# The last three rows of W_down, loaded by GpSimd in nine unequal transfers

## The chip, the cores and the metric

The kernel runs on one core of one Trainium2 chip. The metric is the device time of one execution in microseconds (us). The kernel before takes 383.76 us, the median of three runs (383.7 to 384.0).

## The reference, cut to what matters

One decode step of a transformer layer for 4 sequences, with model width 576: a layer norm, attention of 32 query heads on 16 cached key/value heads over a window of 4096 positions, a residual, a second layer norm, and a gated feed-forward layer of width 4608. What the change touches is the last matrix product of the feed-forward layer:

```python
gate = jnp.einsum("bsd,df->bsf", x, W_gate)
up = jnp.einsum("bsd,df->bsf", x, W_up)
gate = gate * (gate > 0)
h = gate * up
return jnp.einsum("bsf,fd->bsd", h, W_down)   # W_down: 4608 x 576, bf16
```

All arrays are bf16. Keys, values and weights together are 159.6 MB, and each byte is read once.

## The kernel before, in words

The kernel is written engine by engine. A small scheduler (`Sched`, L50 to L100) turns names into semaphore counts: `op` and `dma` wait for the names in `deps` and announce their own. Each engine's program runs in the order in which it is written: `prog_sync` (L267), `prog_pool` (L275), `prog_act` (L299), `prog_dve` (L366) and `prog_pe` (L516). TensorE (PE) records all matmuls under L520, since a helper `mm` issues them.

**Loads.** All large loads stand in one list, `transfers`, and SyncE (SP) issues them in that order on one queue (L268). The order is wq, then 32 pairs of K and V tiles of 2 MB each, then wo, W_gate and W_up, and last W_down. A transfer waits only for the consumers of the part of the SBUF tile `pool` that it overwrites. Each covers all 128 partitions.

**W_down.** Partition p holds 36 rows of W_down, numbered f = 0 to 35, of 576 elements (1152 bytes) each: four groups of nine (`NG` = 4, `JJ` = 9). The list `WD` (L251) cuts the 36 rows into nine transfers, `("wd", 0)` to `("wd", 8)`: two of 9 rows, five of 3 rows, one of 2 rows and one of 1 row. A row over all partitions is 144 KB. They are issued at L256, and their only condition is `"ATTN"`, the last matmul of the output projection, because W_down takes the place of wo in `pool`.

**After the loads.** PE computes gate and up from W_gate and W_up as they land. ScalarE (ACT) applies the relu (L361), VectorE (DVE) multiplies and transposes the product into `hhT` (L507 and L510, names `("HHT", g)` for group g). Then PE takes the W_down transfers in the order of `WD` (L660): for each row f two matmuls of 288 columns, one for each half of the 576 outputs, all into one accumulator bank. The very last one, `"DOWN1"`, releases two copies, one on ACT (L363) and one on DVE (L513), and SP stores the result (L270).

**GpSimd (POOL).** It sets constants at the start and does one maximum over all partitions for each of eight batches of the attention (L295). Behind the eighth its program is empty, and it issues no transfer. ACT issues one small transfer, that of x, at L301.

Of the kernel before, what the change touches and what calls it, by code (L numbers as in the profile page):

```python
# [13 lines left out]
D = 576  # L14
# [7 lines left out]
FC = F // 128  # L22
# [17 lines left out]
JJ = 9  # L40
BIG = 1.5e38
NG = FC // JJ
# [60 lines left out]
def bass_sequential_preLN__sliding_block_cached__glu_gated_reglu__decode_kernel(  # L103
# [12 lines left out]
    with ExitStack() as es:  # L116
        cnt = [0]

        def sb(name, shape, dt):
            return es.enter_context(nc.sbuf_tensor(name, shape, dt))  # L120

        pool = sb("pool", [128, (NKS + NVS) * DUO], BF16)
# [69 lines left out]
        S = Sched()  # L192
# [45 lines left out]
        for g in range(NWO):  # L238
            add(("wo", g), f"wo{g}", g * ROW, ROW, "ATTN",
                lambda e, o, g=g: e.dma_start(out=o,  # L240
                                              in_=A_wo[g * 1024:(g + 1) * 1024, :].rearrange("(p e) n -> p (e n)", e=8)))
# [6 lines left out]
                lambda e, o, W=W: e.dma_start(out=o, in_=W[512:576, :].rearrange("r (u n) -> (r u) n", u=2)))  # L248

        wd_sb = pool[:, 0:FC * D].rearrange("p (g x) -> p g x", g=NG)  # L250
        WD = [(0, 9), (9, 18), (18, 21), (21, 24), (24, 27), (27, 30), (30, 33), (33, 35), (35, 36)]  # L251
        for k, (f0, f1) in enumerate(WD):
            g0, j0 = divmod(f0, JJ)
            g1, nj = (f1 // JJ, JJ) if f1 - f0 >= JJ else (g0 + 1, f1 - f0)
# [2 lines left out]
                                  out=wd_sb[:, g0:g1, j0 * D:(j0 + nj) * D],  # L257
                                  in_=B_W_down[g0 * 128 * JJ:g1 * 128 * JJ, :].rearrange("(g p j) n -> p g (j n)", p=128, j=JJ)[:, :, j0 * D:(j0 + nj) * D])))

        def feat(c):  # L260
            return slice(c // 2 * 256 + c % 2, c // 2 * 256 + c % 2 + 255, 2) if c < 4 else slice(512, D)

        def land(name):
            return ("L",) + (name if isinstance(name, tuple) else (name,))
# [9 lines left out]

        def prog_pool(S):  # L275
            g = "gpsimd"
            S.op(g, lambda e: e.memset(eps_c[:, :], EPS), name="EPS")
            S.op(g, lambda e: e.memset(ident_b[:, :], 0.0), name="P0")
            S.op(g, lambda e: e.memset(qz[:, :, :, :, :].rearrange("p a r c m -> p (a r c m)"), 0.0), name="QZ0")
            S.op(g, lambda e: e.affine_select(out=ident_b[:, :], in_=ident_b[:, :], pattern=[[-1, 128]],  # L280
                                              compare_op=ALU.not_equal, fill=1.0, base=0, channel_multiplier=1),
                 deps=["P0"], name="IDB")
            S.op(g, lambda e: e.memset(ones_f[:, :], 1.0), name="ONES")
            S.op(g, lambda e: e.memset(R_sb[:, :, :, :], 0.0), name="R0")
            S.op(g, lambda e: e.memset(hnT[:, :, :], 0.0), name="HNZ")
            S.op(g, lambda e: e.memset(hn4[:, :, :], 0.0), name="HN4Z")
            S.op(g, lambda e: e.memset(ident_f[:, :], 0.0), name="P1")
            S.op(g, lambda e: e.affine_select(out=ident_f[:, :], in_=ident_f[:, :], pattern=[[-1, 128]],
                                              compare_op=ALU.not_equal, fill=1.0, base=0, channel_multiplier=1),
                 deps=["P1"], name="IDF")  # L290
            for n in range(NBATCH):
                deps = [("EMAX", n)]
                if n >= 2:
                    deps.append(("BIAS", n - 2))
                S.op(g, lambda e, n=n: e.partition_all_reduce(bcm[:, n % 2, :], pmax[:, n % 2, :], 128, bass_isa.ReduceOp.max),  # L295
                     deps=deps, name=("PAR", n))


        def prog_act(S):  # L299
# [216 lines left out]
        def prog_pe(S):  # L516
            t = "tensor"

            def mm(o, l, r, start, stop, deps=(), name=None, skip=False):
                S.op(t, lambda e: e.matmul(o, lhsT=l, rhs=r, start=start, stop=stop, skip_group_check=skip),  # L520
                     deps=deps, name=name, signal=name is not None)

            for k, (src, base) in enumerate(((xn_bf, 0), (x_bf, 32))):
                for c in range(DC):
                    w = 128 if c < 4 else 64
                    last = k == 1 and c == DC - 1
                    S.op(t, lambda e, c=c, w=w, src=src, base=base: e.transpose(  # L527
                        out=tpv[0:w, base + c * 4:base + (c + 1) * 4], in_=src[0:B, feat(c)], identity=ident_b[0:B, 0:B]),
                        deps=["A_XN", "IDB", land("x")] if k == 0 and c == 0 else [], name="TP1" if last else None, signal=last)
            mm(pb[STB][:, 0:B], dup[:, :], x4[:, :], True, True, deps=["D_XNT", "DUP"], name="XDUP")  # L530
            first = True
            for c in range(4):
                s = at[("wq", c // 2)] + (c % 2) * HQ
                for h in range(H):
                    mm(pb[QB][:, h * B:(h + 1) * B], pool[:, s + h * DH:s + (h + 1) * DH], xnT[:, c, :], first, False,
                       deps=[land(("wq", c // 2))] + (["D_XNT"] if first else []) if h == 0 else [], skip=True)
                    first = False
            s = at[("wq", 4)]
            for h in range(H // 2):
                o = pb[QB][:, 0:H * B].rearrange("p (u x) -> p u x", u=2)[:, :, h * B:(h + 1) * B]  # L540
                mm(o, pool[:, s + h * DH:s + (h + 1) * DH], xn4[:, :, :], False, h == H // 2 - 1,
                   deps=[land(("wq", 4)), "XN41"] if h == 0 else [],
                   name="QMM" if h == H // 2 - 1 else None, skip=True)
            for ce in range(4):
                mm(pb[QR][:, ce * 128:(ce + 1) * 128], sel[:, ce, :, :].rearrange("p g k -> p (g k)"), qT_sb[:, :], True, True,
                   deps=["D_QT", "SEL3"] if ce == 0 else [], name="QREP" if ce == 3 else None)
# [55 lines left out]
            for e_ in range(8):  # L602
                mm(sc[:, e_ * 128:(e_ + 1) * 128], S8[:, e_ * 128:(e_ + 1) * 128], oT_all[:, :, :].rearrange("p h b -> p (h b)"), True, True,
                   deps=[("NORM", b) for b in range(B)] + ["S8"] if e_ == 0 else [], name="OSEL" if e_ == 7 else None)
            for g in range(NWO):
                wv = pool[:, at[("wo", g)]:at[("wo", g)] + ROW].rearrange("p (e n) -> p e n", e=8)
                deps = [land(("wo", g))] + (["D_OX"] if g == 0 else [])
                for n in range(DC):
                    w = 128 if n < 4 else 64
                    for e_ in range(8):  # L610
                        last = g == NWO - 1 and n == DC - 1 and e_ == 7
                        mm(pb[WOB][0:w, n * B:(n + 1) * B], wv[:, e_, feat(n)], oX[:, e_, g, :],
                           g == 0 and n == 0 and e_ == 0, last, deps=deps, name="ATTN" if last else None, skip=True)
                        deps = []
# [19 lines left out]
            for c in range(4):  # L634
                if c == 2:
                    residual()
                for u, kind in ((0, "wg"), (1, "wu")):
                    s = at[(kind, c // 2)] + (c % 2) * F
                    deps = [land((kind, c // 2))] + (["N2"] if c == 0 and u == 0 else [])
                    begun = set()  # L640
                    for g, f0, f1, bank, c0 in PARTS:
                        for q in range(4):
# [3 lines left out]
                            deps = []  # L646
                        begun.add(bank)

            for u, kind in ((0, "wg"), (1, "wu")):
                s = at[(kind, 4)]  # L650
                deps = [land((kind, 4)), "HN41"]
                for k, (g, f0, f1, bank, c0) in enumerate(PARTS):
                    for q in range(4):
                        x0 = s + (g % 2) * 4 * JW + q * JW
                        last = k >= 2
                        mm(pb[GUB[u][bank]][32 * q:32 * q + 32, c0:c0 + (f1 - f0) * JJ], hn4[:, g // 2, :], pool[:, x0 + f0 * JJ:x0 + f1 * JJ],
                           False, last, deps=deps, name=(("GATE", "GU")[u], bank) if last and q == 3 else None, skip=True)
                        deps = []

            for k, (f0, f1) in enumerate(WD):  # L660
                deps = [land(("wd", k))]
                for f in range(f0, f1):
                    g, j = divmod(f, JJ)
                    if f % JJ == 0:
                        deps = deps + [("HHT", f // JJ)]
                    for u in range(2):
                        last = f == FC - 1
                        mm(pb[DNB][32 * u:32 * u + B, 0:HD], hhT[:, f, 0:B], wd_sb[:, g, j * D + u * HD:j * D + (u + 1) * HD], False, last,
                           deps=deps, name="DOWN1" if last and u == 1 else None, skip=True)
                        deps = []  # L670

        progs = [("gpsimd", prog_pool), ("sync", prog_sync), ("scalar", prog_act), ("vector", prog_dve), ("tensor", prog_pe)]
        S.begin(False)
        for _, p in progs:
# [33 lines left out]
```

## Time and profile before

| what | value |
|---|---|
| median of three runs | 383.76 us |
| the profiled execution | 383.99 us |
| its span, first to last instruction | 382.2 us |
| read from HBM | 159.58 MB, 418 GB/s over the span |
| PE busy | 287.7 us (75%) |
| DVE busy | 206.5 us (54%) |
| ACT busy | 53.5 us (14%) |
| POOL busy | 8.2 us (2%) |
| the eight maxima on POOL, the last at | 310.38 us |
| "ATTN" releases the W_down transfers at | 347.2 us |

Times within the profile are microseconds from the start of the span. The profiled execution is 0.23 us longer than the median of the runs, and 1.8 us of it lie outside the span. The page shows the core's 16 DMA engines together, as the mean share of time in which they were busy; the trace holds one record for each packet that a DMA engine moved (one partition's piece of a transfer is a packet here), and one for each increment of a transfer's semaphore. A transfer on 128 partitions increments its semaphore 16 times, once for each DMA engine that has moved its part, and the consumer waits for all 16. The records name the queue of a packet but not the number of the DMA engine.

### The profile page before, as it was taken

Reading aid. Unit: us, or ns where it says so; the run is one execution under the profiler, and the core shown is the slowest. Engines: PE = TensorE matmul, PEld = TensorE weight load, DVE = VectorE, ACT = ScalarE, POOL = GpSimd, SP = SyncE. Lnnn points to the kernel's source line nnn. Section 1 sums busy time; section 2 is a strip of 40 time slices with the busy share of each in tenths; the row PEclk is TensorE's granted clock in tenths of the full one; section 3 lists DMA queues with packets and bytes.
Section 4 is the critical chain, followed back from the end, with each engine's and each line's share of the span. In section 5 each row is a group of like instructions: output and inputs, shape, how many; then the busy total and the mean of one; then the engine's idle time right before and its main releaser. Section 6 shows DMA issues by size and latency. Waiting matters only on the chain.

```text
span 382.2 us, 3916 instructions
## 1 busy us (share of the span) xinstructions
PE 287.7 (75%) x1697; PEld 124.5 (33%) x1712; DVE 206.5 (54%) x193; ACT 53.5 (14%) x129; POOL 8.2 (2%) x22
## 2 busy tenths in 40 slices
PE   0069749977997799669967996799589796956565
PEld 0053213322432243224322432243224233344331
DVE  0369789369437854774477548744865442042030
ACT  4021050021102110211021103010300021010020
POOL 4100000000000000000000000000000000000000
PEclk9999988997998799989998999899989996965677
DMA  8999999999999999999999999999999999999994
GB/s 307 434 424 422 436 422 429 431 425 427 426 429 430 424 429 430 425 429 429 429 425 430 425 427 432 424 430 427 427 430 425 427 431 424 419 430 424 420 416 198
DMA packets 12417, 159.84 MB, mean 418 GB/s; under 512 B 1384, under 2 KB 1520, under 8 KB 2672
## 3 DMA queue, kind: packets, MB, share of 16 engines
q1 hardware_dynamic: 12392, 159.59, 98.7%
q8 instruction: 13, 0.21, 0.2%
q14 instruction: 4, 0.03, 0.0%
q10 hardware_dynamic: 8, 0.00, 0.0%
HBM read 159.58 MB, written 0.00 MB: 418 GB/s over the span
## 4 chain that ended last, share of the span: by engine, by line
PE 50%; DVE 18%; issue 16%; ACT 6%; DMA 5%; SPq 3%; POOL 1%; POOLq 0%
PE sc L520 27%; PE pb L520 23%; DVE kT L416 6%; ACT P L344 5%; DMA pool<-in_B_W_down_dram 5%; DVE probT L435 4%; DVE rmx L419 4%; SPq L256 3%; POOL bcm L295 1%; DVE P L477 1%; DVE bias L431 0%; DVE rowsum L440 0%; DVE pmax L422 0%; DVE t L427 0%; DVE bmin L429 0%
## 5 line engine op out<-in xcount | busy, mean ns | idle before, releaser
L416 DVE STREAM_TRANSPOSE kT<-pool 128x2048 f32<-128x2048 f32 x64 | 144.5, 2291 | 54.4 <-DMA pool<-in_A_k_cache_dram 47.6
L520 PE MATMUL sc<-kT,qz 128*128 128x512 bf16 x497 | 133.1, 422 | 48.4 <-DVE kT L416 45.1
L520 PE MATMUL pb<-pool,prob 128*16 128x512 bf16 x512 | 118.5, 391 | 0.0
L520 PEld LDWEIGHTS sc<-kT,qz 128*128 128x128 bf16 x512 | 49.2, 102 | 128.6 <-DVE kT L416 53.2
L520 PEld LDWEIGHTS pb<-pool,prob 128*16 128x16 bf16 x512 | 44.0, 92 | 72.4 <-issue 19.0
L344 ACT ACTIVATE P<-sc,bias 128x512 f32<-128x512 f32 x32 | 22.2, 718 | 176.8 <-DVE bias L431 176.8
L419 DVE TENSOR_REDUCE rmx<-sc 128x2 f32<-128x2048 f32 x8 | 18.3, 2292 | 34.9 <-PE sc L520 34.9
L435 DVE STREAM_TRANSPOSE probT<-P 128x2048 f32<-128x2048 f32 x8 | 18.5, 2312 | 7.9 <-ACT P L344 7.9
L527 PE MATMUL pb<-ident_b,xn_bf 4*128 4x4 bf16 (+1 forms) x5 | 0.4, 175 | 19.6 <-ACT xn_bf L308 19.6
L329 ACT COPY cp<-pb 128x512 f32<-128x512 f32 x8 | 4.7, 585 | 67.9 <-PE pb L520 67.9
L520 PE MATMUL pb<-selT,cp 128*128 128x16 f32 x64 | 8.7, 269 | 4.4 <-ACT cp L329 4.4
L520 PEld LDWEIGHTS pb<-selT,cp 128*128 128x128 f32 x64 | 9.0, 208 | 6.5 <-ACT cp L329 5.4
L351 ACT CAST prob<-probT 128x1024 bf16<-128x1024 f32 x8 | 8.4, 1044 | 19.0 <-DVE rs L438 19.0
L444 DVE RECIPROCAL rs_sb<-pb 128x32 f32<-128x32 f32 x4 | 1.4, 339 | 17.8 <-PE pb L520 17.8
L507 DVE TENSOR_TENSOR P<-pb,P 128x288 bf16<-128x288 f32 (+1 forms) x2 | 0.8, 400 | 17.3 <-PE sc L520 17.3
L520 PE MATMUL pb<-pool,probT 128*4 128x288 bf16 x72 | 6.1, 310 | 5.4 <-DMA pool<-in_B_W_down_dram 5.4
L295 POOL PARTITION_ALL_REDUCE bcm<-pmax x8 | 3.1, 388 | 291.5 <-DVE pmax L422 291.5
L322 ACT COPY qz<-qrep 32x64 bf16<-32x64 bf16 x32 | 7.8, 244 | 7.3 <-DVE qrep L453 7.0
L520 PE MATMUL sc<-oX,pool 128*128 128x4 bf16 (+1 forms) x160 | 5.9, 172 | 3.7 <-DVE oX L480 3.7
L520 PE MATMUL pb<-pool,hnT 128*32 128x288 bf16 (+1 forms) x48 | 4.0, 405 | 6.0 <-DMA pool<-in_B_W_up_dram 6.0
L520 PE MATMUL sc<-pool,hnT 128*32 128x288 bf16 (+2 forms) x112 | 6.8, 366 | 0.6 <-DMA pool<-in_B_W_gate_dram 0.6
L520 PEld LDWEIGHTS sc<-oX,pool 128*128 128x128 bf16 (+1 forms) x160 | 5.8, 114 | 4.0 <-issue 3.9
(107 smaller groups left out, 80.1 us busy)
## 6 DMA issues: line engine op xcount, KB each, us to landing
pool<-in_A_k_cache_dram SPq DMA_DIRECT2D x32, 2048.0 KB, 27.9
pool<-in_A_v_cache_dram SPq DMA_DIRECT2D x32, 2048.0 KB, 25.9
pool<-in_A_wo_dram SPq DMA_DIRECT2D x4, 1152.0 KB, 21.7
pool<-in_B_W_gate_dram SPq DMA_DIRECT2D x2, 2304.0 KB, 24.8
pool<-in_B_W_up_dram SPq DMA_DIRECT2D x2, 2304.0 KB, 27.3
pool<-in_A_wq_dram SPq DMA_DIRECT2D x2, 2048.0 KB, 10.1
pool<-in_B_W_down_dram SPq DMA_DIRECT2D x2, 1296.0 KB, 24.1
pool<-in_B_W_down_dram SPq DMA_DIRECT2D x5, 432.0 KB, 25.8
```

Source lines behind the costliest of these rows:

```text
L256: lambda e, g0=g0, g1=g1, j0=j0, nj=nj: e.dma_start(out=wd_sb[:, g0:g1, j0 * D:(j0 + nj) * D], in_=B_W_down[g0 * 128 * JJ:g1 * 128 * JJ, : ...
L295: S.op(g, lambda e, n=n: e.partition_all_reduce(bcm[:, n % 2, :], pmax[:, n % 2, :], 128, bass_isa.ReduceOp.max), deps=deps, name=("PAR", n))
L322: S.op(a, lambda e, src=src, dst=dst: e.copy(out=dst, in_=src), deps=deps, name=("QZ", n) if g == 3 else None, signal=g == 3)
L329: S.op(a, lambda e: e.copy(out=cp[:, n % 2, :], in_=pb[PVB + n % 2]), deps=deps, name=("CP", n))
L344: S.op(a, lambda e, n=n, th=th, u=u: e.activation(out=P[:, th * 1024 + u:(th + 1) * 1024:2], in_=sc[:, th * 1024 + u:(th + 1) * 1024:2], f ...
L351: S.op(a, lambda e, n=n: e.copy(out=prob[:, n % 2, :, :, :], in_=probT[:, :, 0:NHB].rearrange("p t (r x) -> p r t x", x=4)), deps=deps, na ...
L416: S.op(v, lambda e: e.transpose(out=dst, in_=src), deps=deps, name=("TR", i))
L419: S.op(v, lambda e: e.tensor_reduce(out=rmx[:, n % 2, :], in_=sc[:, :].rearrange("p (x u) -> p u x", u=2), axis=AX.X, op=ALU.max), deps=[( ...
L435: S.op(v, lambda e: e.transpose(out=probT[:, :, :].rearrange("p t j -> p (t j)"), in_=P[:, :]), deps=[("EXP", n, 1)] + ([("CMP", n - 1)] i ...
L444: S.op(v, lambda e: e.reciprocal(out=rs_sb[:, b, :], in_=pb[OB][:, 64 + b * H:64 + (b + 1) * H]), deps=[("SUM", b)], name=("RS", b))
L477: S.op(v, lambda e: e.tensor_reduce(out=oS.rearrange("p (x b) -> p x b", b=B), in_=oM.rearrange("p (x s b) -> p x b s", s=8, b=B), axis=AX ...
L520: S.op(t, lambda e: e.matmul(o, lhsT=l, rhs=r, start=start, stop=stop, skip_group_check=skip), deps=deps, name=name, signal=name is not None)
```

## The change

Rows 33, 34 and 35 of every partition leave SP's list. `WD` now ends with a transfer of rows 30 and 31 and one of row 32, so SP issues eight W_down transfers where it issued nine.

The three rows of a partition lie side by side, 3456 bytes, and POOL loads them behind the eighth maximum, once `"ATTN"` is there. It does so in nine transfers over 4, 17, 2, 46, 2, 34, 2, 19 and 2 neighbouring partitions, which together are the 128. All nine increment one semaphore, and the last carries the name that PE waits for (9 times 16 increments).

PE takes the rows 33 to 35 as the seventh of nine pieces, after rows 27 to 29 and ahead of 30 and 31 and of 32. The last matmul is now that of row 32. The wait for `("HHT", g)` is asked for at every piece; where the engine has already waited for that count nothing is issued.

```diff
-        WD = [(0, 9), (9, 18), (18, 21), (21, 24), (24, 27), (27, 30), (30, 33), (33, 35), (35, 36)]
+        WD = [(0, 9), (9, 18), (18, 21), (21, 24), (24, 27), (27, 30), (30, 32), (32, 33)]
+
+        WDX = (4, 17, 2, 46, 2, 34, 2, 19, 2)
...
         def prog_pool(S):
             g = "gpsimd"
+
+            def last_rows():
+                f0, p0 = FC - 3, 0
+                src = B_W_down[(NG - 1) * 128 * JJ:, :].rearrange("(p j) n -> p (j n)", j=JJ)
+                for k, n in enumerate(WDX):
+                    S.dma(g, lambda e, p0=p0, n=n: e.dma_start(out=pool[p0:p0 + n, f0 * D:FC * D], in_=src[p0:p0 + n, (JJ - 3) * D:JJ * D]),
+                          "wdx", deps=["ATTN"], name=land("wdx") if k == len(WDX) - 1 else None)
+                    p0 += n
+                assert p0 == 128
...
                      deps=deps, name=("PAR", n))
+            last_rows()
...
-            for k, (f0, f1) in enumerate(WD):
-                deps = [land(("wd", k))]
+            order = [(f0, f1, ("wd", k)) for k, (f0, f1) in enumerate(WD)]
+            order.insert(6, (FC - 3, FC, "wdx"))
+            for f0, f1, what in order:
+                deps = [land(what), ("HHT", f0 // JJ)]
                 for f in range(f0, f1):
                     g, j = divmod(f, JJ)
-                    if f % JJ == 0:
+                    if f % JJ == 0 and f > f0:
                         deps = deps + [("HHT", f // JJ)]
                     for u in range(2):
-                        last = f == FC - 1
+                        last = f == order[-1][1] - 1
```

## The prediction

> **What bounds the kernel.** First the page: its slices of DMA and its queues.
>
> ```profile
> span 382.2 us, 3916 instructions
> ...
> DMA  8999999999999999999999999999999999999994
> ...
> q1 hardware_dynamic: 12392, 159.59, 98.7%
> q8 instruction: 13, 0.21, 0.2%
> q14 instruction: 4, 0.03, 0.0%
> q10 hardware_dynamic: 8, 0.00, 0.0%
> ```
>
> The 16 DMA engines are busy from the second slice to the last but one, nearly all with q1, SP's queue. A change can win only by moving fewer bytes or at the two ends. The change moves the same bytes, so the end is what matters. Next, the chain of waits from 340 us on:
>
> ```profile
> 358.78 19.51 DMA pool<-in_B_W_down_dram
> 378.29 0.04 issue
> 378.33 1.62 PE pb L520 x12
> 379.96 0.02 issue
> 379.98 0.45 DVE out_sb L513
> ```
>
> W_down's transfers set the end; PE follows each landing at once. The timeline of the tail shows the landings as starts of PE's groups:
>
> ```profile
> 377.28 0.53 PE L520 MATMUL pb<-pool,probT 128*4 128x288 bf16 x6 [0.53 <-DMA pool<-in_B_W_down_dram]
> 378.33 0.33 PEld L520 LDWEIGHTS pb<-pool,probT 128*4 128x4 bf16 x6 [0.84 <-DMA pool<-in_B_W_down_dram]
> ...
> 379.04 0.10 PEld L520 LDWEIGHTS pb<-pool,probT 128*4 128x4 bf16 x4 [0.38 <-DMA pool<-in_B_W_down_dram]
> 379.40 0.09 PEld L520 LDWEIGHTS pb<-pool,probT 128*4 128x4 bf16 x2 [0.26 <-DMA pool<-in_B_W_down_dram]
> ```
>
> Three rows land 1.05 us after the three before, two rows 0.71 later, one row 0.36 later. Then the DMA view of the last 3.7 us of data:
>
> ```profile
> DMA  8997995994976665667256343333333323222210
> ...
> q1 hardware_dynamic: 391, 0.79, 54.8%
> ```
>
> The share falls from all engines to few long before the last packet: 45% of 16 x 3.7 = 59.2 engine-us, some 26.8, is unused. The trace's 16 increments of the last semaphore are one per engine: 375.77, 375.93, 376.47, 376.65, 376.69, 376.99, 377.32, 377.45, 377.73, 377.74, 378.58, 378.98, 379.10, 379.29, 379.33 and 379.36. Their mean is 377.71, so the last engine is 1.65 us behind an even finish (26.8 / 16 = 1.68 says the same). That is the most that any sharing out could win. The spread is old: 0.8 us after the first transfer, growing where an instruction fetch (q8, q14) falls on one engine: behind the 16 KB fetch at 25.81 us one engine is 1.5 us later for good. It is 3.6 us throughout W_down.
>
> **The change, part by part.**
>
> *Removed from SP's queue:* one 3-row transfer, eight packets of 3456 bytes on every engine. Price: landing to landing 1.05 us, 0.131 a packet. Every engine ends its SP work 1.05 earlier, the latest at 378.31. SP also saves an issue; it issued the last at 362.8, 16.5 us ahead of its landing, so that is worth nothing.
>
> *Added on POOL:* nine issues behind "ATTN" at 347.2. Before shows no transfer by POOL. The bounds are SP's shortest issue, 0.33 us, so 3 us in all, and POOL's longest unexplained pause, 10.4 us ahead of L280, once, plus nine times SP's median, 1.28, so 22 us. Nearer is a small multiple of the first, as POOL's own rows take 0.1 to 0.4. The issues end between 350 and 369; PE asks for these rows at 377.3. That slack of 8 us hides them. Behind them POOL has nothing; its eight maxima come before.
>
> *The shares.* What decides is which engine carries how many of the 128 pieces. A 128-partition transfer gives 8 packets to each of 16 engines. The x transfer, 4 partitions, is the 8 packets of q10, four of data and four of 4 bytes. Both are equal shares over the largest number up to 16 that divides the partitions. By that, 17 and 19 go to one engine each, 46 to two with 23 each, 34 to two with 17 each, and 4 and the 2s give one piece to an engine. So six engines carry 17 to 23 pieces, and the others one or two. The other bound is the evenest split: 17 as 2 on each of nine engines.
>
> [...]
>
> *A late engine:* minus 1.05, plus one piece 0.13, plus nine 4-byte packets of about 0.006 each (their spacing in the trace), 0.05: 379.36 - 0.87 = 378.49. An engine with two pieces: 378.62. *An early engine:* exactly six end by 376.99. With 23, 23, 19, 17, 17, 17 pieces in the order of their ends they finish at 377.79, 377.95, 377.97, 377.88, 377.92 and 378.22, all ahead of 378.49. The sizes fit the lags. Whether they fall on those engines the records don't tell, since they number no engine.
>
> *PE.* The wait for the new piece stands seventh; queued behind it are rows 30 to 32 and the end. Rows 27 to 29 land at 377.24 + 0.18 = 377.42. Six rows then follow without a pause. The windows show the clock:
>
> ```profile
> 374.63:378.04 3.41, 1.66 (x20) 1.00 0.72 286
> 378.04:379.93 1.89, 1.60 (x12) 0.50 0.13 48
> ```
>
> The granted clock is 1.00 and then 0.50, and a row's pair of matmuls starts every 0.12 us at the one and 0.24 at the other. From 377.46, five rows at 0.12, then 0.24 from 378.07: the ninth row starts at 378.79, not at its landing 378.53. Before, it started at 379.49. That gain is 0.70. With the clock full to the end it is 0.87; with it halved from 377.4 on, 377.46 + 8 x 0.24 = 379.38 and 0.1. The drop comes at a step of 3.41 us that need not lie the same way in another run. Two of the three ends lie close, and I take **0.80**, between them. DVE is done with hhT at 372.0, ahead of all this. Copies, store and end (0.45, 0.35 and the rest) move along unchanged.
>
> Sum: 383.99 - 0.80 in the profiled execution; from the median 383.76, **382.96 us**.
>
> **The rivals.**
>
> *1. The bytes are no cheaper elsewhere (no gain).* Every packet costs the same to all engines, 0.611 us for 16 KB, 0.131 for 3456 bytes. These rows fit a limit in the engine, but also one on the receiving partitions, since every large transfer gives an engine the same partitions. Were it the partitions', a late engine's partitions still take eight pieces of 0.131, whoever brings them, and the 1.05 comes back: 383.76, give or take 0.3. For it: nothing here separates the two. Against: engines late after a fetch stay late alone, and the four packets of x, all to partitions 0 to 3, started in pairs 0.002 us apart.
>
> [...]
>
> *2. The large shares fall on late engines (slower).* The place is the last landing. An engine with n pieces ends 0.131 x (n - 8) later than before, so from nine on it is later. The latest with 17 ends at 379.36 + 1.18 + 0.05 = 380.6, with 23 at 381.4; the even split gives the first engines 15, 380.3. That is 1.0 to 2.0 longer; the middle is 17 pieces, 1.2, **385.0 us**. For it: six of sixteen engines end within 0.8 us of the last, and the order of the engines is in no record. Against: the sizes match six early lags.
>
> *3. A second queue costs time at each switch (slower).* After that 16 KB fetch the next SP packet took 1.16 us where 0.61 is usual, 0.55 more. A late engine gets about ten foreign packets in nine bursts; at 0.087 each the gain is gone, at 0.4 it is 3.1 us longer, 386.9. Against it: the fetch, of instructions and not of data, took 1.07 itself, so the 0.55 can be its tail.
>
> *4. POOL is late:* if its transfers need 2.5 us each and 10 to begin, they land after 379, and the kernel is 1 us or more longer.
>
> **How the numbers follow.** Forecast 0.48; rival 1 0.18; rival 2 0.24; rival 3 0.07; rival 4 0.03. A measurement of this kernel tells about 0.2%, 0.77 us, from no change. The forecast's own range is 382.7 to 383.6 (gains of 1.05 to 0.1), with 0.34 beyond 0.2% and 0.14 within. Rival 1 is 0.14 within and 0.04 slower, rival 2 is 0.02 within and 0.22 slower, rivals 3 and 4 slower. Faster 0.34, same 0.30, slower 0.36. Range: below 382.7 I leave out 0.03 of the forecast; it goes up to 385.2, past rival 2's middle, and leaves out its upper quarter (0.06) and rivals 3 and 4 (0.10).
>
> **What would show it.** Right: the increments of the last W_down semaphore spread over about 1 us instead of 3.6, the last near 378.5; a new queue with 128 packets of 3456 bytes; POOL's issues done by 369. Wrong by rival 1: packets that take longer than 0.131 while the new queue runs, and the last increment near 379.3. By rival 2: the spread grows past 3.6. By rival 3: a longer packet behind each new one. By rival 4: PE's seventh piece waits for its landing while the eighth is there. PE in the way: no pause ahead of the last six rows.

## The result, and the profile after

The changed kernel takes 386.73 us (median of six runs, 386.34 to 388.25), the kernel before 383.73 beside it; the ratio is 1.0082 (95% interval 1.0071 to 1.0093). It is 3.0 us slower, where 0.8 us faster was forecast. The profiled execution took 386.34 us, with a span of 384.5.

The page of the changed kernel, with the lines that answer to those of before:

```profile
span 384.5 us, 3924 instructions
...
DMA  8999999999999999999999999999999999999995
...
q1 hardware_dynamic: 12248, 159.15, 98.4%
q0 software_dynamic: 320, 0.44, 0.4%
```

The new queue is q0, GpSimd's. Its 0.44 MB are what q1 lost. The DMA engines show as busy as before; what that share hides is seen below. The chain of waits has the same members at the end, all later:

```profile
354.50 26.37 DMA pool<-in_B_W_down_dram
380.87 0.04 issue
380.91 1.39 PE pb L532 x18
382.31 0.02 issue
382.33 0.45 DVE out_sb L525
```

The timeline of the tail shows that PE still follows the landings:

```profile
378.78 0.21 PEld L532 LDWEIGHTS pb<-pool,probT 128*4 128x4 bf16 x6 [0.80 <-DMA pool<-in_B_W_down_dram]
...
379.85 0.21 PEld L532 LDWEIGHTS pb<-pool,probT 128*4 128x4 bf16 x6 [0.86 <-DMA pool<-in_B_W_down_dram]
...
380.91 0.58 PEld L532 LDWEIGHTS pb<-pool,probT 128*4 128x4 bf16 x12 [0.85 <-DMA pool<-in_B_W_down_dram]
...
381.64 0.09 PEld L532 LDWEIGHTS pb<-pool,probT 128*4 128x4 bf16 x4 [0.15 <-DMA pool<-in_B_W_down_dram]
382.00 0.08 PEld L532 LDWEIGHTS pb<-pool,probT 128*4 128x4 bf16 x2 [0.26 <-DMA pool<-in_B_W_down_dram]
```

The twelve weight loads at 380.91 are rows 27 to 29 and, without a pause, the new rows 33 to 35, which had landed at 367.8. So GpSimd's rows were there in time. What came late is SP's queue. In the DMA view of the last 3.7 us of data, 60.8% is busy now, where it was 54.8%:

```profile
DMA  9899789798878887957775564453443323222111
...
q1 hardware_dynamic: 422, 0.88, 60.8%
```

The fall is as long as before: the 16 increments of the last semaphore run from 378.23 to 381.96, a spread of 3.73 us (3.60 before), with a mean of 380.46 (377.71 before). Nothing was levelled: taken in order, each of the 16 increments is later, by 2.28 us or more and by 2.75 on average. A limit of the engines alone can't do that. The bytes are the same and only shared out otherwise, so the mean of the ends would stay, but for some 0.1 us of 4-byte packets (q0 has 218 of them, of 0.009 us each, for 16 engines).

Where it was lost is seen in the last increments of SP's transfers. W_up's first part lands at 352.81 (352.86 before), W_gate's second part at 359.93 (358.36), W_up's second part at 367.56 (363.95), the first W_down transfer at 373.52 (369.90), and rows 27 to 29 at 380.87 (377.24). So 3.6 us are lost between 353 and 368, while q0 has packets (351.7 to 367.1), and nothing after. The shorter list then gives back its 1.05.

The table of stretches has, after the length, PE's busy time and count, its granted clock, the busy share of the DMA engines, and GB/s. Before:

```profile
356.00:360.00 4.00, 2.44 (x34) 0.80 0.97 411
360.00:364.00 4.00, 0.00 (x1) 0.62 0.97 402
```

After:

```profile
356.00:360.00 4.00, 1.80 (x18) 0.78 1.02 329
360.00:364.00 4.00, 0.65 (x20) 0.65 1.00 321
```

The engines are as busy as before and move 20% less. The packet records say how: of SP's 221 packets of 18432 bytes that start between 351.6 and 367.2 us, 173 take more than 0.72 us, up to 1.18. In before one of 226 did, and the others took about 0.69. What lies above 0.69 is some 34 us of engine time. Over the whole run, the packets of q0 and q1 together take 43.6 us more than q1's in before, which is 2.73 for each of 16 engines, next to the 2.75 by which the increments are later.

The sizes of q0's packets tell the shares. They are 43 packets of 6912 bytes (two pieces together) and 42 of one piece (3456, or 3460 with a word behind it). That fits blocks of a sixteenth of the partitions, rounded up to whole ones, so one, two or three pieces to an engine: 17 gives eight packets of two and one single, 46 gives fifteen of two, each with a single, and one single, 34 eleven and twelve, 19 nine and one, and 4 and the four 2s twelve singles. With 17 or 23 pieces on one engine pairs would make 55 packets of two, one behind another on few engines. Of the fifteen of the 46 partitions, fourteen start within 0.9 us, and each takes 0.26 us or more.

### The profile page after: what moved, and what is told of

It reads as the page before. It is cut to its first block, busy times and chain, and to the rows that moved or that the text cites. A ratio compares the mean times of both kernels' runs of the same rounds, so it can differ in the third digit from the quotient of the medians.

```text
span 384.5 us, 3924 instructions
## 1 busy us (share of the span) xinstructions
PE 284.4 (74%) x1697; PEld 123.2 (32%) x1712; DVE 206.3 (54%) x193; ACT 53.5 (14%) x129; POOL 13.1 (3%) x31
## 4 chain that ended last, share of the span: by engine, by line
DMA 43%; PE 26%; DVE 19%; issue 5%; ACT 4%; SPq 2%; POOL 1%; POOLq 0%
DMA pool<-in_A_k_cache_dram 36%; PE pb L532 14%; PE sc L532 12%; DVE kT L428 11%; DMA pool<-in_B_W_down_dram 7%; ACT P L356 3%; DVE probT L447 2%; DVE rmx L431 2%; SPq L258 2%; DVE P L489 1%; POOL bcm L306 0%; DVE P L485 0%; DVE sel L388 0%; ACT cp L341 0%; ACT prob L363 0%
## 5 line engine op out<-in xcount | busy, mean ns | idle before, releaser
L532 PE MATMUL sc<-kT,qz 128*128 128x512 bf16 x497 | 131.7, 416 | 51.7 <-DVE kT L428 48.2
L532 PE MATMUL pb<-pool,prob 128*16 128x512 bf16 x512 | 117.2, 388 | 0.0
L532 PEld LDWEIGHTS sc<-kT,qz 128*128 128x128 bf16 x512 | 48.1, 101 | 131.7 <-DVE kT L428 60.9
L532 PE MATMUL pb<-pool,probT 128*4 128x288 bf16 x72 | 5.3, 286 | 4.9 <-DMA pool<-in_B_W_down_dram 4.9
```

## The experiments

The working theory after the result (A): pieces that are written to partitions which another engine is serving at that time slow both. Its rivals: (B) every burst of a second queue costs an engine a fixed time; (C) bytes on GpSimd's queue are dear in themselves; (D) the reading side does it. In each edit the rest is the changed kernel, unless it says otherwise. Ratios are to the kernel before on the same chip, with 95% intervals.

**One transfer of 128 partitions.**

```diff
-        WDX = (4, 17, 2, 46, 2, 34, 2, 19, 2)
+        WDX = (128,)
```

> The changed kernel with its nine GpSimd transfers joined into one of 128 partitions, so that each DMA engine gets eight pieces, those of the partitions that it always serves. In the changed kernel 33.8 engine-us were lost in SP's 18432-byte packets, which took up to 1.18 us instead of 0.69 on all engines while the pieces ran. Theory A (pieces written to partitions that another engine is serving at the time slow both engines): no piece crosses now, so the loss goes and the time is that of before, 383.7 us, give or take 0.3; SP's 18432-byte packets stay at 0.69. Theory B (each burst of a second queue costs every engine a fixed time; 2.75 us over nine bursts, 0.31 each): one burst, 384.0. Theory C (any bytes on GpSimd's queue are dear, 0.34 us more for each of 128 pieces): as the changed kernel, 386.4 or more.

Measured: 383.81 us, ratio 0.9998 (0.9988 to 1.0007). The same bytes on the same queue, taken by PE at the same place, cost nothing. The same stretches, then the queues from 348 to 368 us:

```profile
356.00:360.00 4.00, 1.99 (x42) 0.93 1.02 428
360.00:364.00 4.00, 0.37 (x8) 0.50 0.97 406
```

```profile
q1 hardware_dynamic: 756, 7.97, 94.7%
q0 software_dynamic: 80, 0.44, 5.3%
```

q0's 64 data packets have 0.265 us for two pieces, SP's stay at 0.69, and GB/s is that of before. The last increment is at 379.40 with a mean of 377.74. C falls: neither the queue nor the order of PE's pieces is the cause. It is the cut into nine, be it the number of transfers or the partitions that they go to. B's 384.0 is too near to be told apart here.

**Eight transfers of 16 neighbouring partitions.**

```diff
+        WDX = (16,) * 8
```

> The three rows by GpSimd in eight transfers of 16 neighbouring partitions, one piece for each engine in each transfer, so all engines carry eight pieces, but nearly all of other engines' partitions and crowded on 16 neighbours. Theory A: at least the loss of the changed kernel, which had the same 128 pieces: 386.5 or more, with SP's 18432-byte packets beyond 1 us. Theory B: eight bursts, 8 x 0.31 = 2.4: 386.2. Theory C: 386.4.

Measured: 387.34 us, ratio 1.0085 (1.0059 to 1.0111); mean of the last increments 380.66, 2.95 us later than before. The DMA view from 348 to 368 us, in 40 slices of 0.5 us, shows what happens:

```profile
DMA  9977997939596969593969199939999896989999
GB/s 479 479 332 332 553 406 316 555 94 530 182 491 198 456 219 417 175 484 124 470 219 500 51 523 306 417 131 486 364 309 339 272 403 184 468 341 385 383 412 442
```

From 352 to 362 us the rate falls to between 51 and 306 in every other slice and rises above 400 in the next; with one transfer of 128 partitions it is between 295 and 553 throughout. Swings alone are no loss, since the slices are short: the eight transfers of the next experiment swing from 154 to 673 and lose little. What counts is the mean, 318 GB/s from 356 to 360 us, where one transfer of 128 partitions has 428:

```profile
356.00:360.00 4.00, 2.24 (x22) 0.75 0.97 318
360.00:364.00 4.00, 0.96 (x20) 0.68 0.98 328
```

**Eight transfers of 128 partitions, a slice of 432 bytes of each.**

```diff
+                for k in range(8):
+                    c0 = k * 216
+                    S.dma(g, lambda e, c0=c0: e.dma_start(out=pool[:, f0 * D + c0:f0 * D + c0 + 216], in_=src[:, (JJ - 3) * D + c0:(JJ - 3) * D + c0 + 216]),
...
```

> The three rows by GpSimd in eight transfers of all 128 partitions with 432 bytes of a partition each: the same bytes and the same number of bursts as the eight of 16 partitions, but every engine serves its own partitions. Theory A: 383.8, with a little for 64 small packets per engine in place of eight (0.3 at most). Theory B: 386.2, as its sister with 16 partitions. Theory C, if it is by bytes: 386.4; if by packets, far more.

Measured: 384.18 us, ratio 1.0012 (1.0002 to 1.0023). Eight bursts of eight pieces each, in packets of 3456 bytes, cost 0.3 us on the mean (378.02), where its sister with 16 partitions lost 2.95. B falls as the main cause. What makes the 0.3 is open: 73 of SP's 219 packets of 18432 bytes between 351.6 and 367.2 us take more than 0.72 us, most of them 0.74 to 0.78.

**No second queue: one of SP's own transfers cut into eight of 16 partitions** (kernel before).

```diff
+            for p0, p1 in ([(p, p + 16) for p in range(0, 128, 16)] if k == 6 else [(0, 128)]):
```

> The kernel before, with one edit: the seventh W_down transfer (rows 30 to 32), still on SP's queue and at its old place, is issued as eight transfers of 16 neighbouring partitions. No second queue and nothing by GpSimd. Theory A: each small transfer has 16 pieces for 16 neighbouring partitions, which were the share of two engines, or of four if neighbours are shared out in fours; its 16 pieces then take 0.131 x 8 or x 4 instead of 0.131, at the end of the queue and with engines that come 3.6 us apart, so 1 to 3 us longer than before: 384.7 to 386.7. Theories B and C: no second queue, so as before, 383.7, give or take 0.2.

Measured: 385.79 us, ratio 1.0048 (1.0031 to 1.0066). SP's packets of 3456 bytes, 0.135 us each in before, take up to 0.35. So neither GpSimd nor a second queue is needed. C is out, and B as the main cause.

**Which side: every eighth partition, at both ends and at one.**

```diff
-                for k, n in enumerate(WDX):
-                    S.dma(g, lambda e, p0=p0, n=n: e.dma_start(out=pool[p0:p0 + n, f0 * D:FC * D], in_=src[p0:p0 + n, (JJ - 3) * D:JJ * D]),
+                for k in range(8):
+                    S.dma(g, lambda e, k=k: e.dma_start(out=pool[k:128:8, f0 * D:FC * D], in_=src[k:128:8, (JJ - 3) * D:JJ * D]),
```

The other two kernels have `16 * k:16 * k + 16` in place of `k:128:8` for the partitions written, or for those read.

> GpSimd's eight transfers again have 16 pieces each, one for each engine, but now every eighth partition instead of 16 neighbours, at both ends. The neighbours took a last landing from 379.4 to 382.5 us, on average 2.95 us later, 0.37 for each transfer. If a group of four neighbouring partitions shares one limit, 16 neighbours are four groups with four pieces each: 4 x 0.131 - 0.131 = 0.39 lost in each, which fits. [...] Theory A2 (the limit is that of eight neighbouring partitions, or of four alone): one piece for each limit, nothing lost: 383.8. Theory C (any partial transfer on GpSimd's queue is dear): as the neighbours, 387.3.

> As the eight transfers to 16 neighbouring partitions, but each reads every eighth row group of the last quarter of W_down, so that partitions get other partitions' rows (rows 33 to 35 are permuted, and the sums over them come out otherwise). Theory A (the writing side decides): 387.3 us, as with neighbours at both ends. Theory D (the reading side decides, neighbouring pieces of memory read at once): as pool_far.

> The opposite: each transfer writes every eighth partition but reads 16 neighbouring row groups (rows 33 to 35 are permuted over the partitions). [...] Theory D (the reading side): 387.3, as with neighbours at both ends.

| written | read | us | ratio | mean of the last increments |
|---|---|---|---|---|
| 16 neighbours | 16 neighbours | 387.34 | 1.0085 (1.0059 to 1.0111) | 380.66 |
| 16 neighbours | every eighth | 387.04 | 1.0077 (1.0054 to 1.0099) | 381.18 |
| every eighth | 16 neighbours | 385.80 | 1.0045 (1.0030 to 1.0061) | 379.51 |
| every eighth | every eighth | 385.66 | 1.0044 (1.0028 to 1.0060) | 379.77 |

The time follows what is written, and what is read makes no difference beyond the intervals. D falls. Every eighth partition still costs 1.9 us, where A2 had no loss. By A1, the theory that four neighbours and the four that lie 32 further on share one limit (not shown by these four runs), two pieces meet in each of eight groups: an estimated 0.131 lost in each transfer, 1.05 in all, 384.8 us for both kernels that write every eighth. This was missed too, by 0.9 to 1.0 us (0.8 to 1.0 on the mean). Some 0.3 of this may be what eight transfers cost when no piece crosses; the rest stays open. It may be that crossing costs something even without crowding; no run here gives 16 engines one foreign piece for each group. Which partitions share a limit is left to the lone transfers below.

**Are engines relieved by having their pieces taken off? ScalarE, 16 transfers of eight partitions.**

```diff
+        WDX = (8,) * 16
...
+                    S.dma(a, lambda e, p0=p0, n=n: e.dma_start(out=pool[p0:p0 + n, f0 * D:FC * D], in_=src[p0:p0 + n, (JJ - 3) * D:JJ * D]),
...
                  deps=["D_VARC2"], name="A_STD2")
+            last_rows()
```

> The three rows leave SP's queue and come by ScalarE in 16 transfers of eight neighbouring partitions, issued behind its square root at 349.5 us. By the equal shares that the x transfer shows on this queue, eight engines get 16 pieces each (eight more than in the kernel before, 1.05 us) and the other eight none (eight fewer, 1.05 us less). This asks whether an engine is relieved when its pieces are taken off it. If the limit is the engine's (the prediction's forecast): the eight relieved engines end 1.05 earlier, so eight of the 16 increments of the last semaphore come 1.05 earlier than in the kernel before, the last eight 1.05 later; the first increment at or before 375, the mean 377.7 or, with the blocking that the eight transfers to 16 partitions showed, a little more. If the limit is the partitions' (rival 1): relieved engines lose what others write to their partitions and end no earlier than before: no increment before 375.7, and the mean rises, since the writing engines' own partitions stand idle meanwhile. The time in either case 384 to 387 us.

Measured: 387.63 us, ratio 1.0095 (1.0075 to 1.0115). q10 carries 128 packets of 3456 bytes and 128 more increments than before, eight for each of the 16 transfers: eight engines. The last increments come at 377.94, 378.48, 379.42 and from there to 383.18, with a mean of 380.89. None is earlier than the first of before, 375.77, and in order each is later by 2.17 us or more. If it is the same eight engines each time, which the records don't tell, the other eight have 1.05 us less to do, and nothing of that is seen. But a delay of 3.18 on the mean would cover it. The run shows no relief, and doesn't prove that there can be none; so the limit itself was then measured alone.

**The disputed limit by itself** (kernel before, with eight transfers behind its result, each alone).

```diff
+            for k, (p1, step) in enumerate(((2, 1), (33, 32), (65, 64), (5, 4), (4, 1), (13, 4), (16, 1), (128, 1))):
+                n = len(range(0, p1, step))
+                S.dma("sync", lambda e, p1=p1, step=step, n=n: e.dma_start(
+                    out=pool[0:p1:step, 0:2 * F], in_=B_W_gate[0:2 * n, :].rearrange("(p u) n -> p (u n)", u=2)),
+                    f"probe{k}", deps=[last], name=("PROBE", k))
```

> The kernel before, and behind its stored result eight more transfers on SP's queue, each alone, since each waits for the one ahead: 18432 bytes of W_gate to each of partitions 0 and 1; 0 and 32; 0 and 64; 0 and 4; 0 to 3; 0, 4, 8 and 12; 0 to 15; 0 to 127. The x transfer's equal shares give each engine one packet in the first seven (2, 4 or 16 engines) and eight in the last. Nothing else moves, so a packet is slowed only by the others of its own transfer. If the limit is the engine's (the prediction's forecast): every packet takes 0.69 us as in the rest of the kernel, a little more for a first one. If it is that of a group of partitions (rival 1, theory A1 with the group of four and the four 32 further on): 1.38 for 0 and 1, and for 0 and 32; 0.69 for 0 and 64, 0 and 4, and for 0, 4, 8, 12; 2.76 for 0 to 3 and for 0 to 15; 0.69 in the last. Groups of eight neighbours: 1.38 for 0 and 4. Groups of four alone: 0.69 for 0 and 32. The run is longer than the kernel before by the eight transfers, some 30 us.

One execution took 414.67 us, 384.17 for the kernel before. The expectation was put in terms of the packets' own durations, and it failed in these: 0.68 to 1.21 us in the four pairs and 0.92 to 1.71 in the next three, and nowhere the 1.38 or 2.76 against 0.69 that a group called for. (In the last transfer, to all partitions, most packets take 0.69, as expected.) The landings tell. Where the partitions are 0 and 64, 0 and 4, or 0, 4, 8, 12, the last increment comes 0.3 us after the end of the last packet; for 0 and 1 and for 0 and 32 it comes 0.9 to 1.0 us after it. So the end of a packet's record is not yet its landing. From the trace, up to the last increment:

| partitions | engines | from the start of the first packet, us | of the last, us |
|---|---|---|---|
| 0 and 64 | 2 | 1.05 | 1.04 |
| 0 and 4 | 2 | 1.34 | 1.20 |
| 0, 4, 8, 12 | 4 | 1.36 | 1.28 |
| 0 and 32 | 2 | 1.88 | 1.66 |
| 0 and 1 | 2 | 2.13 | 1.67 |
| 0 to 3 | 4 | 3.07 | 2.99 |
| 0 to 15 | 16 | 3.24 | 2.94 |

In the last column, a second packet for the same group adds 0.5 to 0.6 us, and three more add 1.7 to 1.9. Sixteen engines on partitions 0 to 15, by A1 four groups with four packets each, need as long as four engines on partitions 0 to 3 (2.94 and 2.99 us). Partition 32 counts with partition 0 (1.66 us), and partitions 4 and 64 don't (1.20 and 1.04). These transfers agree with A1 in the grouping, for the partitions tried: 0 to 15, 32 and 64. For all others it was not shown. Three more packets in 1.7 to 1.9 us are 28 to 32 GB/s, not far from one engine's own rate (18432 / 0.69 = 26.7 GB/s). Each row is one transfer of one execution.

**What this makes of the loss.** The engines had no pause to spare: their busy share was 0.97 to 1.04 in before's 4 us stretches from 344 to 372 us. So while a foreign piece queues for a crowded group, the engine's own group would stand idle. This is argued; no record shows the idle group. What follows is an estimate that takes A1 for all 128 partitions and 0.131 us for a piece. A transfer of 16 neighbours takes 4 x 0.131 instead of 0.131; eight of them lose 3.1 us, and 2.95 were measured. In the changed kernel the largest number of pieces for one group is 4, 4, 2, 8, 2, 5, 2, 4 and 2 in its nine transfers, 33 in all, 33 x 0.131 = 4.3; an even spread would take 8 x 0.131 = 1.05. The difference is 3.3, and 2.75 were measured. For these two it fits to half a microsecond, but it isn't a model that was proved. It gives too little for every eighth partition (1.05 against 1.8 and 2.1), and too much for SP's cut transfer at the end of the queue (3.1 against a mean of 1.4) and for ScalarE's 16 transfers (16 x 4 x 0.131 - 1.05 = 7.3 against 3.2). What is shown is that blocks of partitions cost time by where they are written; the size of the loss is not yet a sum.

## Why the prediction was wrong

- **What bounds the kernel:** right. W_down's landings set the end, before and after.
- **One transfer off SP's queue, 1.05 us:** right in size. The delay is 3.6 us up to rows 27 to 29 and 2.60 at the last landing, 1.05 less (rounded).
- **POOL's nine issues between 350 and 369:** right. They took 4.97 us in all, from 347.63. (POOL's own rows in before don't all take 0.1 to 0.4 us, as the prediction says: that of L279 takes 3.52. Nothing hung on it.)

```profile
347.63 4.97 POOL L284 DMA_DIRECT2D pool<-in_B_W_down_dram  x9 [36.81 <-PE sc L532]
```

- **The shares:** wrong. The forecast carried the equal shares of SP's transfers of 128 partitions and of x's 4 over to GpSimd's: 17 to 23 pieces for six engines. No run shows these. GpSimd's packets, 43 of 6912 bytes and 42 of one piece, are near the other bound, two or three pieces to an engine. On ScalarE's queue eight partitions did go to eight engines, by the eight increments of each transfer, which both bounds give.
- **"A late engine: minus 1.05":** this is the step on which the forecast stood, and it failed apart from the shares. It took the limit to be the engine's, so that a piece taken off a late engine would be 0.131 us gained there and 0.131 spent elsewhere. Shared out in any way, that leaves the mean of the last increments at 377.71; it went to 380.46. The lone transfers show another limit of about the same rate (28 to 32 GB/s, and 26.7 for an engine): two engines that write to one group land 1.88 and 2.13 us after the first packet's start, and 1.05 and 1.34 where the groups differ. By that, a piece that another engine brings uses up the same time of the late group and is no relief. ScalarE's 16 transfers show none, though there the delay would hide it.
- **Rival 1 (no gain)** had this limit right and its consequence wrong. That an engine serves the same partitions in every large transfer was assumed, and no record tells it; the transfers of all 128 partitions on GpSimd's queue, with 0.0 and 0.4 us lost, only agree with it. It priced a crossing piece at nothing beyond the 1.05 coming back. In fact SP's own packets grew longer too: all in all, the packets took 43.6 us more of engine time. By the account above, the engine that brings a piece is held up, and its own partitions with it. Its argument against, that the four packets of x to partitions 0 to 3 started in pairs, was no argument: the starts and ends of single packets don't show the limit, as the lone transfers say.
- **Rival 2 (late engines get more)** had the right side and, with the even split, nearly the right shares, but not the cause. Its even split ends at 380.3, and the last landing came at 381.96. The spread hardly grew (3.60 to 3.73 us); all the increments were late.
- **Rival 3 (switching)** named the sign that was seen, longer packets beside the new ones. One transfer of 128 partitions switches as well, and costs nothing, and eight of them cost 0.4 us; SP's cut transfer doesn't switch, and costs 2.0 us.
- **PE in the way:** not so. The clock was 1.00 to the end here (378.04 to 382.30 us), and PE paused for each of the last two landings.
- **The range** ended at 385.2: rivals 3 and 4 and the dear end of rival 2 had been left outside. The prediction had a limit of the engine and one of the partitions side by side, and the measured 0.131 us for 3456 bytes, 26.4 GB/s, fitted both. With two limits of nearly one size, what a collision costs both sides should have been worked out.

## What to carry to other kernels

Where the DMA engines are busy all the time, as here (a share of 0.97 to 1.04), cut a transfer along the bytes of a partition, not along the partitions: eight slices over 128 partitions cost 0.4 us, eight blocks of 16 partitions 3.6. The change lent the unused time of engines to the partitions of others, and lost 3.0 us. So before one levels engines, a few lone transfers with two packets each tell whose limit it is: they landed after 1.05 to 1.34 us with a limit for each, and after 1.88 to 2.13 with one for both. A busy share near 100% says nothing about this; read GB/s beside it (from 356 to 360 us a share of 0.97 went with 411 GB/s before, and 1.02 with 329 after).

## What the runs showed of the hardware that was not expected

- Packets to partitions 0 and 1, and to 0 and 32, held each other up: two of 18432 bytes landed after 2.13 and 1.88 us, and after 1.05 and 1.34 where they went to 0 and 64, and to 0 and 4.
- By the sizes of its packets, GpSimd's queue split 17 partitions over nine engines and 46 over sixteen, and it put two neighbouring pieces into one packet of 6912 bytes.
- A second queue started late beside SP's full one: GpSimd's first packet moved 4.0 us after its issue began (347.63 to 351.66), 4.1 with one transfer of 128 partitions, and ScalarE's 3.4 us after (349.68 to 353.04).
- A packet's record can end 0.3 to 1.6 us before the last increment of its transfer (0 and 64; 0 to 3).
